# Infini-attention beside a spectral filter on one core: a causal mask moved from VectorE to TensorE, and element-wise work moved to GpSimd

## Chip, core and metric

One Trainium2 chip, one of its cores. The metric is the device time of one execution in microseconds (us), the median of several. Five engines work side by side, each through its own instructions in order: TensorE (PE; its weight loads are shown apart as PEld), VectorE (DVE), ScalarE (ACT), GpSimd (POOL) and SyncE (SP, which here only issues DMAs). PE writes to PSUM, whose tiles DVE and ACT read and GpSimd does not.

## The reference

Two independent parts, put side by side in the output of 2048 x 1152 floats.

Part A is an attention of 32 heads of 18 channels over 2048 tokens, in 4 segments of 512, with a compressive memory:

```
q,k,v = heads of x@wq, x@wk, x@wv          # 2048 x 576 each
for s in 4 segments:
    logits = qs@ks^T * 18**-0.5 + mask     # mask: -1e9 where key > query
    a_dot  = softmax(logits) @ vs
    pq     = phi(qs)                       # t>0: t+1, else exp(t)
    a_mem  = (pq@M) / (pq@z + 1e-6)
    outs  += g*a_mem + (1-g)*a_dot         # g = sigmoid(beta), per head
    M += phi(ks)^T@vs;  z += sum of phi(ks)
A = concat(outs) @ wo
```

Part B is `irfft2(rfft2(x) * (w_r + i w_i))` of a 2048 x 576 array.

## The kernel before

The program is emitted in the order in which it is to run (a manual schedule): the order of each engine's instructions is that of the Python code, and generators that `yield` are advanced in turn to interleave the work. The parts, by time in the profile: forward transform of B and projections of A (up to about 287 us), inverse transform of B with the first attention steps between (to about 388), the attention loop (to about 755), and an end with the last combination and output projection.

**Attention.** A *step* `t` is one head of one segment, 128 of them; four steps are a *round* `k` (`k,hh=divmod(t,4)`), 32 rounds; eight rounds are a segment. The softmax needs the maximum of each query row ahead of the exponential. So a step has two halves, which the loop runs ten steps apart:

- `s1(t)` (L595 to L616) computes the scores of the four blocks of 128 queries, each against the keys up to its own block: 128, 256, 384 and 512 columns, with four matmuls (L602). The tiles are `pa` (128 and 384 columns), `pc` (512) and `pb` (256), all from one PSUM pool of three buffers, `s1`. `red` (L604 to L607) then takes, on DVE, the row maxima of each of the four pieces: one custom operation adds the mask (zero, and -1e30 above the diagonal of the last 128 columns), takes the maximum and throws the sums away (`junk`); a second small instruction writes the accumulator to a column of `mg`, 128 x 4 heads x 4 blocks.
- `mpath(k)` (L617 to L632), once a round, turns `mg` into rows: a PE transpose into an `s1` buffer (`mt`, L621), two ACT copies (`mf`, and its bf16 high part `mts`, L626 and L627), a DMA from GpSimd's queue that puts the high part into a row of the stacked queries `Qs` (`put(0)`, L623), on DVE the low part (L630), and `put(1)`. In this way the maximum is subtracted by the matmul that makes the exponent.
- `s2(t)` (L633 to L658) computes the scores again, transposed, with the maxima subtracted (L641, L645, L646, L650, three PSUM tiles), and the exponentials on ACT (L642, L647, L651). At the last head of a round four selects on GpSimd (L653) clear what lies above the diagonal.
- `pv(k,jj)` (L659 on, matmul L668) multiplies the probabilities by the values, with a column of ones that gives the row sums. `u_dmas` writes both to DRAM, the row sums to `rD`.

In one pass of the loop (L828 to L867), the order is: two DMAs of waiting queues; first tile of `s1(t+10)`, first of `s2(t)`, second of `s1`, second of `s2`; `pv`; at hh=3 the low part of `mpath`; third tile of `s1`; at hh=2 the transpose of `mpath(k+2)`; third tile of `s2`; at hh=2 the ACT copies and `put(0)`; then one step of the `lane` (reciprocals) and 1.2 steps of the background list.

**Background.** `recip` (L686) loads 128 x 128 row sums (or memory denominators, `eps`), and on DVE takes the reciprocal (L695), multiplies by the gate (L696), rounds to a high part (L698) and subtracts (L699, low part); it stores both and loads them as 64 x 512. It runs seven times, the last after the loop. `den` and `mem1` compute the memory terms. `combine(g)` (L749) handles a segment's five tiles of up to 126 x 512: PE spreads the reciprocals over rows (`pb`, L765, one PSUM buffer `post`), DVE multiplies (L768, L770) and, but for the first segment, adds the memory term (L771); two passes later ACT rounds to a high part `oh` (L760) and DVE takes the low part `ol` (L761). `oproj(g)` multiplies by the output weights: eight groups of fifteen matmuls (L786) in the same PSUM buffer `post`, each evicted by ACT (L788), with a store for each two. `combine` of the first three segments lies in the loop, that of the last behind it, and it loads its tiles (`ux`, L748) through SP's queue, behind the stores of the projection before.

Of the kernel before, what the change touches and what calls it, by code (L numbers as in the profile page):

```python
# [5 lines left out]
F32=mybir.dt.float32; F32R=mybir.dt.float32r  # L6
AF=mybir.ActivationFunctionType; OP=mybir.AluOpType
# [325 lines left out]
BF=mybir.dt.bfloat16  # L333
# [34 lines left out]
class ATT:  # L368
# [174 lines left out]
    def att_setup(s,cp):  # L543
        nc,io=s.nc,s.io
        s.Qs=[cp.tile([128,8,512],BF,name=f"Qs{i}") for i in range(3)]
        s.Ks=[cp.tile([128,8,512],BF,name=f"Ks{i}") for i in range(4)]
        for i in range(4): nc.gpsimd.dma_start(s.Ks[i][108:110].rearrange("p h c -> p (h c)"),io["neg1"])
        s.mask=cp.tile([128,512],F32,name="mask"); nc.sync.dma_start(s.mask,io["mask"])
        bt=cp.tile([128,1],F32,name="bt"); nc.sync.dma_start(bt,io["beta"])
        e=cp.tile([128,1],F32,name="be"); s.gt=cp.tile([128,1],F32,name="gt"); s.g1=cp.tile([128,1],F32,name="g1")  # L550
        nc.scalar.activation(e,bt,AF.Exp,scale=-1.0)
        nc.vector.tensor_scalar(e,e,1.0,None,op0=OP.add)
        nc.vector.reciprocal(s.gt,e)
        nc.vector.tensor_scalar(s.g1,s.gt,-1.0,1.0,op0=OP.mult,op1=OP.add)
        d=lambda n,sh,dt: s.dp.tile(sh,dt,name=n)
        s.uD=[d(f"uD{i}",[576,512],F32) for i in range(4)]
        s.rD=[d(f"rD{i}",[32,512],F32) for i in range(4)]
        s.dD=[None]+[d(f"dD{i}",[32,512],F32) for i in range(1,4)]
        s.rrD=[d(f"rrD{i}",[64,512],F32) for i in range(4)]
        s.rdD=[None]+[d(f"rdD{i}",[64,512],F32) for i in range(1,4)]  # L560
# [34 lines left out]
    def s1(s,t):  # L595

        nc=s.nc; k,hh=divmod(t,4); n,qd=divmod(k,2); h=4*qd+hh
        Q,K=s.Qs[n%3],s.Ks[n%4]; tp=s.sm
        assert (n,0) in s.loaded and (n,1) in s.loaded,(t,n)
        if hh==0: s.mg[k]=tp.tile([128,4,4],F32,name="mg")  # L600
        def mm(out,i):
            nc.tensor.matmul(out,Q[:108,h,128*i:128*i+128],K[:108,h,:128*(i+1)],start=True,stop=True)  # L602
        def red(src,i):
            w=128*(i+1)  # L604
            junk=tp.tile([128,512],BF,name="junk",bufs=1)
            nc.vector.tensor_tensor_reduce(out=junk[:,:w],in0=src,in1=s.mask[:,512-w:],scale=1.0,scalar=-3.0e38,  # L606
                op0=OP.add,op1=OP.max,accum_out=s.mg[k][:,hh,i:i+1])  # L607
        pa=s.ps1.tile([128,512],F32,name="s1",tag="s1")
        mm(pa[:,:128],0); mm(pa[:,128:],2); red(pa[:,:128],0); red(pa[:,128:],2)
        yield  # L610
        pc=s.ps1.tile([128,512],F32,name="s1",tag="s1")
        mm(pc,3); red(pc,3)
        yield
        pb=s.ps1.tile([128,256],F32,name="s1",tag="s1")
        mm(pb,1); red(pb,1)
        yield  # L616
    def mpath(s,k):  # L617

        nc=s.nc; n,qd=divmod(k,2); Q=s.Qs[n%3]
        pt=s.psm.tile([128,512],F32,name="mt",tag=s.mtag)[:16,:128]  # L620
        nc.tensor.transpose(pt,s.mg.pop(k).rearrange("p h i -> p (h i)"),s.ident)  # L621
        mt=s.sm.tile([16,2,128],BF,name="mts",bufs=1)
        def put(a): nc.gpsimd.dma_start(Q[108+a:109+a,4*qd:4*qd+4].rearrange("p h (i c) -> p (h i) c",c=128),mt[:,a])  # L623
        yield
        mf=s.sm.tile([16,128],F32,name="mf",bufs=1)
        nc.scalar.copy(mf,pt)  # L626
        nc.scalar.copy(mt[:,0],mf)  # L627
        put(0)
        yield
        nc.vector.tensor_tensor(mt[:,1],mf,mt[:,0],op=OP.subtract)  # L630
        put(1)
        yield  # L632
    def s2(s,t):  # L633
# [51 lines left out]
        return L  # L685
    def recip(s,src,dst,gate,eps,load):  # L686
        nc=s.nc; tp=s.tp
        x=tp.tile([128,128],F32,name="rx",bufs=1)
        nc.sync.dma_start(x,src.rearrange("h (b c) -> (h b) c",b=4))
        yield  # L690
        yield
        yield
        if eps: nc.vector.tensor_scalar(x,x,1e-6,None,op0=OP.add)
        y=tp.tile([128,128],F32,name="ry",bufs=1)
        nc.vector.reciprocal(y,x)  # L695
        nc.vector.tensor_scalar(y,y,gate,None,op0=OP.mult)  # L696
        w=tp.tile([128,2,128],F32R,name="rw",bufs=1)
        nc.vector.tensor_copy(w[:,0],y)  # L698
        nc.vector.tensor_tensor(w[:,1],y,w[:,0].bitcast(F32),op=OP.subtract)  # L699
        nc.sync.dma_start(bass.AP(tensor=dst.tensor,offset=dst.offset,ap=[[128,128],[32*512,2],[1,128]]),w.bitcast(F32))  # L700
        yield
        yield
        r=tp.tile([64,512],F32R,name=load,bufs=1)
        nc.sync.dma_start(r.bitcast(F32),dst)
        s.rc[load]=r
        yield
# [42 lines left out]
    def combine(s,g):  # L749

        nc=s.nc; tp=s.tp; xs=s.ux
        s.oh=[None]*5; s.ol=[None]*5
        for u in range(3): s.ux_load(g,u)
        yield
        yield
        for t in range(7):
            if t>1:
                u=t-2; r=126 if u<4 else 72; x=s.am[u]
                s.oh[u]=tp.tile([126,512],F32R,name="oh",bufs=5); s.ol[u]=tp.tile([126,512],F32R,name="ol",bufs=5)
                nc.scalar.copy(s.oh[u][:r],x[:r])  # L760
                nc.vector.tensor_tensor(s.ol[u][:r],x[:r],s.oh[u][:r].bitcast(F32),op=OP.subtract)  # L761
            if t<5:
                r=126 if t<4 else 72; x=xs[t]
                pb=s.ps.tile([126,512],F32,name="pb",tag="post")
                nc.tensor.matmul(pb[:r],s.sel[:,t,:r],s.rc["rr"],start=True,stop=True)  # L765
                if g==0:
                    s.am[t]=tp.tile([126,512],F32,name="am",bufs=5)
                    nc.vector.tensor_tensor(s.am[t][:r],x[:r],pb[:r],op=OP.mult)  # L768
                else:
                    nc.vector.tensor_tensor(x[:r],x[:r],pb[:r],op=OP.mult)  # L770
                    nc.vector.tensor_tensor(s.am[t][:r],x[:r],s.am[t][:r],op=OP.add)  # L771
                if t<2: s.ux_load(g,t+3)
            yield
    def oproj(s,g):
# [15 lines left out]
                yield  # L790
    def begin(s,sm,sp,ps1):
        s.sm,s.sp,s.ps1=sm,sp,ps1
        s.mg={};s.m2={};s.P={};s.vs={};s.rc={};s.am={};s.pq={};s.ux={};s.loaded=set()
    def prologue(s):

        for n in range(2):
# [12 lines left out]
    def attention(s,tp,ps):  # L809
        s.tp,s.ps,s.psm,s.mtag=tp,ps,s.ps1,"s1"  # L810
        def steps(gen,i):
            for _ in range(i):
                try: next(gen)
                except StopIteration: return
        m=None
# [12 lines left out]
        for t in range(133):  # L828
            k,hh=divmod(t,4); n,qd=divmod(k,2); g=k//8
            if hh==0 and qd==0:  # L830
                if n+2<16: q+=s.stack_dmas(n+2,0)
                if n+3<16: q+=s.stack_dmas(n+3,1)
                if n+2<16: q.append(lambda n=n: s.load_v(n+2))
            st=t%32
            if 16<=t<21: s.pq_load(1,t-16)
            if t==34: bg.append(s.den(1,lane))
            if st==10 and g>0:
                def ln(g=g):
                    yield from s.recip(s.rD[g-1],s.rrD[g-1],s.g1,False,"rr")
                    bg.append(s.combine(g-1))  # L840
                    for u in range(5 if g<4 else 0): bg.append(s.mem1(g,u))
                    if g<3: bg.append(s.den(g+1,lane))
                    bg.append(s.oproj(g-1))
                lane.append(ln())
            a=s.s1(t+10) if t+10<128 else iter(())
            b=s.s2(t) if t<128 else iter(())
            if q: q.pop(0)()
            if qu: qu.pop(0)()
            steps(a,1)
            steps(b,1)  # L850
            steps(a,1)
            steps(b,1)
            if 4<=t-1<132: s.pv((t-5)//4,(t-5)%4)
            if hh==3 and m is not None: steps(m,1); m=None
            steps(a,1)
            if hh==2 and k+2<32: m=s.mpath(k+2); next(m)
            steps(b,1)
            if hh==2 and m is not None: steps(m,1)
            if t>=8 and t%4==0:
                s.pv_out((t-8)//4)  # L860
                if t%8==4: qu+=s.u_dmas((t-12)//8)
            for l in list(lane):
                try: next(l)
                except StopIteration: lane.remove(l)
            if q: q.pop(0)()
            if qu: qu.pop(0)()
            run_bg(1.2)  # L867
# [108 lines left out]
```

## Time and profile before

| | |
|---|---|
| median of 3 runs | 826.8 us (824.0 to 826.88) |
| profiled execution | 820.21 us, span of its instructions 818.2 us |
| mean granted TensorE clock | 0.960 |
| busy in the span | PE 727.3, DVE 611.9, ACT 472.3, POOL 181.0 us |
| masked maxima (L606) | 512 operations, 251.3 us, and 512 accumulator reads, 42.4 us |

How to read it: a row of the timeline gives start, duration, engine, line, operation, output <- inputs with shapes, and in brackets how long the engine had been idle and what ended that. Matmuls are pipelined, so their durations hold some latency and overlap; the distance between two starts says what one costs in a stream. In the view by windows, a stretch of the span has for each engine its busy time and the number of instructions. A wait is given as engine, line and tile, then what it waited for, with the sum, the number and the longest.

### The profile page before, as it was taken

Reading aid. Unit: us, or ns where it says so; the run is one execution under the profiler, and the core shown is the slowest. Engines: PE = TensorE matmul, PEld = TensorE weight load, DVE = VectorE, ACT = ScalarE, POOL = GpSimd, SP = SyncE. Lnnn points to the kernel's source line nnn. Section 1 sums busy time; section 2 is a strip of 40 time slices with the busy share of each in tenths; the row PEclk is TensorE's granted clock in tenths of the full one; section 3 lists DMA queues with packets and bytes.
Section 4 is the critical chain, followed back from the end, with each engine's and each line's share of the span. In section 5 each row is a group of like instructions: output and inputs, shape, how many; then the busy total and the mean of one; then the engine's idle time right before and its main releaser. Section 6 shows DMA issues by size and latency. Waiting matters only on the chain.

```text
span 818.2 us, 14656 instructions
## 1 busy us (share of the span) xinstructions
PE 727.3 (89%) x4751; PEld 489.2 (60%) x4751; DVE 611.9 (75%) x1687; ACT 472.3 (58%) x996; POOL 181.0 (22%) x340
## 2 busy tenths in 40 slices
PE   5998999999999969997988988899988999978856
PEld 4887788797897958895333333335542345523645
DVE  5999877895878779986788888886778767792040
ACT  2665894846846534444777755666555665657111
POOL 2110001001001164441553331331312231323000
PEclk9999999999999989999999989999996999989969
DMA  8883434653534778735576556564463644310221
GB/s 305 264 253 116 158 139 152 223 176 119 196 120 168 255 160 204 223 124 143 146 182 144 123 125 163 132 153 122 115 167 92 156 120 120 115 37 17 61 86 58
DMA packets 82496, 121.27 MB, mean 148 GB/s; under 512 B 9368, under 2 KB 49430, under 8 KB 82284
## 3 DMA queue, kind: packets, MB, share of 16 engines
q1 hardware_dynamic: 74836, 104.29, 44.2%
q0 software_dynamic: 7584, 16.05, 6.7%
q8 instruction: 38, 0.62, 0.3%
q14 instruction: 38, 0.31, 0.1%
HBM read 81.75 MB, written 38.35 MB: 147 GB/s over the span
## 4 chain that ended last, share of the span: by engine, by line
PE 60%; DVE 21%; ACT 8%; issue 6%; DMA 3%; SPq 1%; POOL 0%; DVEq 0%; ACTq 0%
PE pj L440 10%; PE po L786 8%; DVE junk L606 8%; PE s L602 8%; PE pv L668 7%; PE pjv L440 7%; PE i L292 3%; PE i L303 3%; PE s L641 2%; PE s L645 2%; PE pn L735 2%; PE pm L497 1%; DMA Qs<-qkD 1%; PE s L650 1%; DVE eo L123 1%
## 5 line engine op out<-in xcount | busy, mean ns | idle before, releaser
L606 DVE CUSTOM_DVE_ANT_0 junk<-s,mask 128x128 bf16<-128x128 f32 (+3 forms) x512 | 251.3, 491 | 71.6 <-PE s L602 27.1
L602 PE MATMUL s<-Ks,Qs 108*128 108x128 bf16 (+3 forms) x512 | 138.2, 313 | 19.5 <-DVE mg L606 16.2
L602 PEld LDWEIGHTS <-Qs 108*128 108x128 bf16 x512 | 47.1, 100 | 114.4 <-issue 100.9
L668 PE MATMUL pv<-P,vs 128*32 128x512 f32 (+3 forms) x1024 | 100.0, 463 | 1.0 <-issue 0.8
L642 ACT ACTIVATE P<-s 128x512 f32<-128x512 f32 x128 | 76.8, 600 | 41.5 <-PE s L641 34.7
L623 POOL DMA_DIRECT2D Qs<-mts x64 | 31.7, 496 | 247.3 <-ACT mts L627 184.3
L651 ACT ACTIVATE P<-s 128x256 f32<-128x256 f32 x128 | 49.1, 383 | 64.2 <-PE s L650 60.1
L647 ACT ACTIVATE P<-s 128x512 f32<-128x512 f32 x128 | 76.3, 596 | 7.5 <-PE s L646 5.6
L653 POOL TENSOR_SCALAR_AFFINE_SELECT P<-P 128x512 f32<-128x512 f32 x128 | 77.0, 641 | 14.2 <-ACT P L642 13.8
L440 PE MATMUL pj<-xh,wqkh 128*128 128x512 f32 x180 | 71.2, 395 | 0.5 <-ACT Z L151 0.5
L440 PE MATMUL pj<-xh,wqkl 128*128 128x512 f32 x180 | 71.1, 395 | 0.0
L440 PE MATMUL pj<-xl,wqkh 128*128 128x512 f32 x144 | 61.8, 429 | 0.0
L641 PE MATMUL s<-Qs,Ks 110*128 110x512 bf16 x128 | 51.2, 400 | 3.6 <-ACT P L642 2.8
L202 DVE TENSOR_TENSOR Z<-t,t 128x290 f32<-128x290 f32 (+1 forms) x96 | 53.0, 598 | 0.2
L292 PE MATMUL i<-civ,Y 128*128 128x256 f32 (+1 forms) x288 | 44.4, 308 | 9.4 <-DVE T L320 5.3
L202 DVE TENSOR_TENSOR t<-Z 128x580 f32<-128x580 f32 x64 | 48.0, 788 | 0.2
L440 PE MATMUL pjv<-wvh,xh 128*128 128x288 f32 x160 | 48.1, 303 | 0.0
L292 PEld LDWEIGHTS i<-civ,Y 128*128 128x128 f32 (+1 forms) x288 | 39.8, 199 | 11.7 <-DVE T L320 6.3
L440 PE MATMUL pjv<-wvl,xh 128*128 128x288 f32 x160 | 46.2, 295 | 0.0
L645 PE MATMUL s<-Qs,Ks 110*128 110x384 bf16 x128 | 43.5, 340 | 0.1
L606 DVE DVE_READ_ACCUMULATOR2_ANT mg<- 128x1 f32 x512 | 42.4, 83 | 0.1
L788 ACT COPY ob<-po 128x288 f32<-128x288 f32 x32 | 12.7, 398 | 48.3 <-PE po L786 48.1
(140 smaller groups left out, 1518.7 us busy)
## 6 DMA issues: line engine op xcount, KB each, us to landing
qkD<-sp SPq DMA_DIRECT2D x36, 384.0 KB
Qs<-qkD SPq DMA_DIRECT2D x96, 144.0 KB
Ks<-qkD SPq DMA_DIRECT2D x96, 144.0 KB
xin<-xb SPq DMA_DIRECT2D x16, 384.0 KB
cfw<-cfw POOLq DMA_DIRECT2D x16, 384.0 KB, 4.4
civ<-civ POOLq DMA_DIRECT2D x16, 384.0 KB, 7.1
vs<-vD SPq DMA_DIRECT2D x16, 330.0 KB
vD<-vt SPq DMA_DIRECT2D x16, 311.0 KB
```

The source lines that it names most:

```text
L202: v.tensor_tensor(o,a,b,op=op)
L292: nc.tensor.matmul(p[:m,k],Y[i][:,q,c*128:c*128+m],cc[:,hl,o:o+256],start=n==0,stop=n==5)
L440: s.nc.tensor.matmul(out,a,b,start=i==0,stop=i==len(L)-1)
L602: nc.tensor.matmul(out,Q[:108,h,128*i:128*i+128],K[:108,h,:128*(i+1)],start=True,stop=True)
L606: nc.vector.tensor_tensor_reduce(out=junk[:,:w],in0=src,in1=s.mask[:,512-w:],scale=1.0,scalar=-3.0e38, op0=OP.add,op1=OP.max,accum_out=s.m ...
L641: nc.tensor.matmul(p0,kk(0),q(0),start=True,stop=True)
L642: nc.scalar.activation(P[0][:,hh],p0,AF.Exp,scale=SC)
L645: nc.tensor.matmul(p1[:,:384],kk(1),q(128),start=True,stop=True)
L647: nc.scalar.activation(P[1][:,hh],p1,AF.Exp,scale=SC)
L653: sel=lambda x,pat: nc.gpsimd.affine_select(out=x,in_=x,pattern=pat+[[1,128]],compare_op=OP.is_ge,fill=0.0,base=0,channel_multiplier=-1)
L668: nc.tensor.matmul(s.pvt[32*hh:32*hh+32,128*j:],vt[:,j,19*h:19*h+32],mv[0][:,hh,mv[1]],start=jj==0,stop=jj==3,skip_group_check=True)
L786: nc.tensor.matmul(ps,a[t][:r,c],b[:r,t,w],start=i==0,stop=i==14)
```

## The change

1. `s1`: the score matmuls for the 384 and the 128 columns are each followed by a matmul of an identity (`idb`) with the triangle mask (`tri`, both bf16, 128 x 128), accumulated on the diagonal block. The two DVE operations on `pa` become one plain reduction, which writes the maximum of each of its four 128-column blocks to `mx`: three belong to the 384-wide piece, one to the 128-wide. The other two maxima stay as they are.
2. `mpath`: two small DVE operations in front of the transpose bring `mx` into `mg`. The low part moves from DVE to GpSimd. In the loop the transpose, the copies and `put(0)` move from hh=2 to hh=3 of the round, where they follow the four selects in GpSimd's queue, and the low part with `put(1)` from hh=3 to hh=0 of the next.
3. `recip`: works in place; multiplication and rounding go to ACT, one pass later, and the subtraction to GpSimd.
4. `combine`: the addition of the memory term and the low part go to GpSimd.

```diff
@@ att_setup
+        s.tri=cp.tile([128,128],BF,name="tri"); nc.scalar.copy(s.tri,s.mask[:,384:])
+        s.idb=cp.tile([128,128],BF,name="idb"); nc.scalar.copy(s.idb,s.ident)
@@ s1
-        if hh==0: s.mg[k]=tp.tile([128,4,4],F32,name="mg")
+        if hh==0: s.mg[k]=tp.tile([128,4,4],F32,name="mg"); s.mx[k]=tp.tile([128,4,4],F32,name="mx")
...
-        mm(pa[:,:128],0); mm(pa[:,128:],2); red(pa[:,:128],0); red(pa[:,128:],2)
+        for o,w,i in ((0,384,2),(384,128,0)):
+            mm(pa[:,o:o+w],i)
+            nc.tensor.matmul(pa[:,o+w-128:o+w],s.idb,s.tri,start=False,stop=True,skip_group_check=True)
+        nc.vector.tensor_reduce(out=s.mx[k][:,hh],in_=pa.rearrange("p (b c) -> p b c",c=128),axis=mybir.AxisListType.X,op=OP.max)
@@ mpath
+        mx=s.mx.pop(k)
+        nc.vector.tensor_reduce(out=s.mg[k][:,:,2:3],in_=mx[:,:,:3],axis=mybir.AxisListType.X,op=OP.max)
+        nc.vector.tensor_copy(s.mg[k][:,:,0:1],mx[:,:,3:])
         nc.tensor.transpose(pt,s.mg.pop(k).rearrange("p h i -> p (h i)"),s.ident)
...
-        nc.vector.tensor_tensor(mt[:,1],mf,mt[:,0],op=OP.subtract)
+        nc.gpsimd.tensor_tensor(mt[:,1],mf,mt[:,0],op=OP.subtract)
@@ recip
+        w=tp.tile([128,2,128],F32R,name="rw",bufs=1); y=w[:,1].bitcast(F32)
+        nc.sync.dma_start(y,src.rearrange("h (b c) -> (h b) c",b=4))
...
-        nc.vector.reciprocal(y,x)
-        nc.vector.tensor_scalar(y,y,gate,None,op0=OP.mult)
-        w=tp.tile([128,2,128],F32R,name="rw",bufs=1)
-        nc.vector.tensor_copy(w[:,0],y)
-        nc.vector.tensor_tensor(w[:,1],y,w[:,0].bitcast(F32),op=OP.subtract)
+        nc.vector.reciprocal(y,y)
+        yield
+        nc.scalar.activation(y,y,AF.Copy,scale=gate)
+        nc.scalar.copy(w[:,0],y)
+        nc.gpsimd.tensor_tensor(w[:,1],y,w[:,0].bitcast(F32),op=OP.subtract)
@@ combine
-                nc.vector.tensor_tensor(s.ol[u][:r],x[:r],s.oh[u][:r].bitcast(F32),op=OP.subtract)
+                nc.gpsimd.tensor_tensor(s.ol[u][:r],x[:r],s.oh[u][:r].bitcast(F32),op=OP.subtract)
...
-                    nc.vector.tensor_tensor(s.am[t][:r],x[:r],s.am[t][:r],op=OP.add)
+                    nc.gpsimd.tensor_tensor(s.am[t][:r],x[:r],s.am[t][:r],op=OP.add)
@@ attention
-            if hh==3 and m is not None: steps(m,1); m=None
+            if hh==0 and m is not None: steps(m,1); m=None
             steps(a,1)
-            if hh==2 and k+2<32: m=s.mpath(k+2); next(m)
+            if hh==3 and k+2<32: m=s.mpath(k+2); next(m)
             steps(b,1)
-            if hh==2 and m is not None: steps(m,1)
+            if hh==3 and m is not None: steps(m,1)
```

More of the change, by code (lines that the diff above doesn't have):

```diff
@@ L687, in recip @@
         nc=s.nc; tp=s.tp
-        x=tp.tile([128,128],F32,name="rx",bufs=1)
-        nc.sync.dma_start(x,src.rearrange("h (b c) -> (h b) c",b=4))
+        w=tp.tile([128,2,128],F32R,name="rw",bufs=1); y=w[:,1].bitcast(F32)
+        nc.sync.dma_start(y,src.rearrange("h (b c) -> (h b) c",b=4))
         yield
@@ L692, in recip @@
         yield
-        if eps: nc.vector.tensor_scalar(x,x,1e-6,None,op0=OP.add)
-        y=tp.tile([128,128],F32,name="ry",bufs=1)
-        nc.vector.reciprocal(y,x)
-        nc.vector.tensor_scalar(y,y,gate,None,op0=OP.mult)
-        w=tp.tile([128,2,128],F32R,name="rw",bufs=1)
-        nc.vector.tensor_copy(w[:,0],y)
-        nc.vector.tensor_tensor(w[:,1],y,w[:,0].bitcast(F32),op=OP.subtract)
+        if eps: nc.vector.tensor_scalar(y,y,1e-6,None,op0=OP.add)
+        nc.vector.reciprocal(y,y)
[3 more added lines that the diff above has]
+        nc.gpsimd.tensor_tensor(w[:,1],y,w[:,0].bitcast(F32),op=OP.subtract)
         nc.sync.dma_start(bass.AP(tensor=dst.tensor,offset=dst.offset,ap=[[128,128],[32*512,2],[1,128]]),w.bitcast(F32))
@@ L792, in begin @@
         s.sm,s.sp,s.ps1=sm,sp,ps1
-        s.mg={};s.m2={};s.P={};s.vs={};s.rc={};s.am={};s.pq={};s.ux={};s.loaded=set()
+        s.mg={};s.mx={};s.m2={};s.P={};s.vs={};s.rc={};s.am={};s.pq={};s.ux={};s.loaded=set()
     def prologue(s):
```

## Prediction

> **What bounds the kernel now.** I read the page first (shares, then the chain that ended last), then a table by stage, then single lines of the timeline. A "step" is one head in the main loop, a "round" four steps.
>
> ```profile
> PE 727.3 (89%) x4751; PEld 489.2 (60%) x4751; DVE 611.9 (75%) x1687; ACT 472.3 (58%) x996; POOL 181.0 (22%) x340
> ...
> PE 60%; DVE 21%; ACT 8%; issue 6%; DMA 3%; SPq 1%; POOL 0%; DVEq 0%; ACTq 0%
> ```
>
> PE leads the chain, DVE is second. Which of them binds changes with what runs beside the attention, so the loop (389 to 739 us) has to be cut into stretches of whole rounds. Columns: stretch, busy time of each engine, PEclk the granted clock.
>
> ```profile
> core 0: us, PE busy (x) PEld busy (x) DVE busy (x) ACT busy (x) POOL busy (x), PEclk, DMA share, GB/s
> ...
> 479.00:528.90 49.90, 41.16 (x270) 15.78 (x268) 41.72 (x152) 30.65 (x66) 13.88 (x25) 0.90 0.55 139
> 528.90:564.60 35.70, 33.97 (x242) 14.79 (x241) 27.75 (x109) 23.59 (x52) 10.16 (x19) 1.00 0.56 133
> 564.60:579.30 14.70, 12.89 (x104) 8.18 (x102) 10.83 (x36) 8.25 (x19) 3.37 (x6) 1.00 0.33 92
> 579.30:604.90 25.60, 25.21 (x193) 15.31 (x191) 18.00 (x73) 14.75 (x34) 6.72 (x12) 0.93 0.56 152
> 604.90:636.70 31.80, 25.85 (x140) 9.06 (x141) 26.44 (x84) 16.91 (x37) 7.28 (x13) 0.79 0.49 129
> 636.70:673.70 37.00, 34.92 (x251) 15.74 (x249) 26.91 (x106) 24.07 (x54) 10.12 (x18) 1.00 0.55 131
> 673.70:687.50 13.80, 11.98 (x98) 7.24 (x96) 10.86 (x36) 7.83 (x18) 3.37 (x6) 1.00 0.36 95
> 687.50:712.10 24.60, 23.96 (x192) 14.44 (x190) 17.90 (x70) 15.29 (x34) 6.41 (x12) 1.00 0.48 132
> 712.10:739.00 26.90, 20.16 (x125) 6.82 (x123) 24.11 (x59) 15.82 (x36) 7.08 (x13) 0.87 0.17 48
> ```
>
> Three kinds. **PE-bound**: the stretches from 528.9, 579.3, 636.7 and 687.5, ten rounds in 122.9 us with PE busy 94 to 98% (memory products and output projection). **DVE-bound**: those from 479.0, 604.9 and 712.1, eight rounds in 108.6 us, PE busy 75 to 82% (reciprocals and combination on DVE). The two single rounds between I leave unchanged. **Plain**: the nine rounds before 479; their length is the distance of two first P·V groups in the chain:
>
> ```profile
> 429.35 1.04 PE pv L668 x8
> 439.21 1.04 PE pv L668 x8
> ```
>
> 9.86 us, 2.465 a step. Is that DVE? A step's four masked maxima have 1280 columns:
>
> ```profile
> 430.46 0.69 DVE L606 CUSTOM_DVE_ANT_0 junk<-s,mask 128x512 bf16<-128x512 f32 x1
> ...
> 431.31 0.42 DVE L606 CUSTOM_DVE_ANT_0 junk<-s,mask 128x256 bf16<-128x256 f32 x1
> ```
>
> Start to start the 512-wide one takes 0.85. If all four fill the step, a fixed part a and a part b per column follow from 4a+1280b=2.465 and a+512b=0.85: b=1.22 ns, a=0.23 us. So the pair of 128 and 384 columns costs 2a+512b=1.08, the 256-wide 0.54, and DVE has no time left: plain rounds are DVE's.
>
> **The change, part by part.**
>
> *One plain maximum for two masked ones.* Cost of a plain 512-element operation by the distance to an independent next one:
>
> ```profile
> 786.90 0.69 DVE L771 TENSOR_TENSOR am<-ux,am 126x512 f32<-126x512 f32 x1
> 787.51 0.68 DVE L761 TENSOR_TENSOR ol<-am,oh 126x512 fp32r<-126x512 f32 x1
> ```
>
> 0.61. The trace shows no plain reduction; bounds 0.61 and 0.85, I take 0.61, since it writes no accumulator. Saved: 1.08-0.61=0.47 a step. Added per round: a reduction of 12 elements and a copy of 4, nearest row
>
> ```profile
> L552 DVE TENSOR_SCALAR be<-be x1: 153/153/153, 292.4 to 292.4; 128x1 f32<-128x1 f32 x1
> ```
>
> so 0.3 for both. DVE's plain round becomes 9.86-1.88+0.3=8.3.
>
> *Two mask matmuls a step on PE.* In the rows below 128+384 columns in two matmuls take 0.23 to the next start, 512 in one 0.22:
>
> ```profile
> 563.62 0.39 PE L602 MATMUL s<-Ks,Qs 108*128 108x128 bf16 x2
> 563.85 0.38 PE L641 MATMUL s<-Qs,Ks 110*128 110x512 bf16 x1
> 564.07 0.38 PE L602 MATMUL s<-Ks,Qs 108*128 108x512 bf16 x1
> ```
>
> So columns count and the extra weight load hides: 0.055 each (bounds 0 and 0.23), 0.43 a round. Where PE waits for DVE it is free; where PE binds it is paid.
>
> *The new wait, which I hold to be the heart of it.* The transpose of the maxima (mt) today comes at hh=2 of a round and reads maxima written a step earlier. It moves to hh=3, directly behind the fourth score matmul of that step (256 columns) on PE, and on DVE the reduction and copy that feed it stand behind that step's three maxima. PE, in order, then stands until DVE has finished the whole step; behind it wait the 256-wide probability matmul, its exponential, the selects and the next step. Today:
>
> ```profile
> PEld mt L621 <- DVE mg L606: 14.9, 20, 3.1
> ```
>
> 14.9 us in 20 of 32 places (another 10 us before the matmul itself), in DVE-bound rounds, where PE has time. The new wait in a round where DVE isn't behind, from a PE-bound step:
>
> ```profile
> 558.72 0.38 PE L602 MATMUL s<-Ks,Qs 108*128 108x512 bf16 x1
> ...
> 559.60 0.28 PE L602 MATMUL s<-Ks,Qs 108*128 108x256 bf16 x1
> ```
>
> The 512 columns stream until 558.93; a matmul's result reaches DVE some 0.4 after:
>
> ```profile
> 564.05 0.29 DVE L606 CUSTOM_DVE_ANT_0 junk<-s,mask 128x128 bf16<-128x128 f32 x1 [0.54 <-PE s L602]
> ```
>
> (563.62, 128 columns, to 564.05). So DVE starts at 559.3, ends the 512-wide at 560.15, the 256-wide at 560.7, reduction and copy at 561.0; PE, ready at 559.72, goes on at about 561.1: **1.4 us**. Bounds: nothing if DVE's work were done, 2.4 (a full step) if DVE is a step behind.
>
> What PE needs for a round without the rest: in one PE-bound round, with the 30 projection matmuls of it below,
>
> ```profile
> 662.00:673.70 11.70, 11.70 (x99) 7.24 (x97) 8.16 (x34) 7.61 (x18) 3.37 (x6) 1.00 0.40 86
> ```
> ```profile
> 662.00:673.70 11.70, 4.73 (x30) 4.11 (x30) 1.00 0.40 86
> ```
>
> 11.70-4.11=7.6. Hence:
> - Plain: 7.6+0.43+1.4 plus the first maximum waiting for PE afterwards, about 9.7 against 9.86: nine rounds give **-1** (bounds -7, DVE alone at 9.0; +6, the wait at 2.4).
> - PE-bound: +0.43+1.4 a round, less some 0.3 where DVE ends a piece of them today: ten rounds **+15** (bounds +4 and +24).
> - DVE-bound: PE's busy 87.2 holds about 1.1 a round of matmul ends behind which it waits; floor 87.2-9+8x1.83+2 (a wait for a load that stays)=95 against 108.6: **-14** (bounds -24 and -5). DVE itself loses 0.47 a step, ten additions, fifteen low parts and three operations of each reciprocal, and falls under that floor.
>
> *The prologue* holds ten of the steps beside the inverse transform: 4.7 us of DVE, mostly under PE: **-1.5** (bounds -5, +3).
>
> *Additions and low parts on GpSimd.*
>
> ```profile
> L575 POOL TENSOR_TENSOR wol<-ob,woh 126x576 fp32r<-126x576 f32 x5 | 7.0, 1408 | 5.7 <-ACT woh L574 5.7
> ```
>
> 1.25 us for 512 elements (bounds 0.69 as on DVE, 1.41). 25 of them in the loop are 31 us on an engine with some 3.4 us a round; the selects can stand behind two of them, but P·V comes two steps later: +2 (bounds 0, 15). The rows of maxima are also later: transpose a step later, and both DMA issues now stand behind the 2.4 us of selects. About 1 (ACT) + 2.4 + 0.5 + 0.3 + 0.5, and then
>
> ```profile
> DMA to landing us min/median/max: 1.5/3.7/7.2
> ```
>
> 8.4 us with the median, 11.9 with the longest, against four steps, 9.7: some rounds wait: +3 (bounds 0, 12). Together **+5**.
>
> [...]
>
> ```profile
> 735.87 2.88 DVE L761 TENSOR_TENSOR ol<-am,oh 72x512 fp32r<-72x512 f32 x1 [0.85 <-ACT oh L760]
> ```
>
> (2.88 beside the selects instead of 0.69). [...] Moving such operations off DVE gains a few of these stalls; that is in the -14.
>
> *The end*, on the path whole:
>
> ```profile
> 770.86 0.40 ACT L788 COPY ob<-po 128x288 f32<-128x288 f32 x1 [2.38 <-PE po L786]
> ```
> ```profile
> 771.60 0.95 DVE L695 RECIPROCAL ry<-rx 128x128 f32<-128x128 f32 x1 [16.34 <-DMA rx<-rD]
> ```
> ```profile
> 779.99 5.99 SPq L748 DMA_DIRECT2D ux<-uD  x5
> ```
> ```profile
> 782.68 0.69 DVE L770 TENSOR_TENSOR ux<-ux,pb 126x512 f32<-126x512 f32 x1 [9.21 <-DMA ux<-uD]
> ```
> ```profile
> 791.47 0.62 ACT L760 CAST oh<-am 72x512 fp32r<-72x512 f32 x1 [1.30 <-DVE am L771]
> ```
>
> ACT now scales and rounds the last reciprocal, in its queue before the fifth projection eviction (770.86). It must wait for 772.55, plus two small operations, 773.2; with one PSUM buffer PE waits too, the last store and the loads queued behind it on SP (779.99) slide by 2.3. Then five additions and five low parts run one after the other on GpSimd: the fifth addition is eighth, 0.75+8x1.25=10.8 after the first product, against 8.8 today (782.68 to 791.47): with its hand-overs 2.3 more. **+4.6** (bounds +1, +7).
>
> Sum: -1+15-14-1.5+5+4.6=+8.1. The profiled execution took 820.2 (span 818.2), so 828; the median of the three runs is 826.8, 0.8% above it. I carry the difference over: **834 us**.
>
> **The rivals.**
> - *DVE is done when PE arrives* (faster). If the transpose's wait stays below 0.6 us, plain rounds go to 9.0 (-8), PE-bound pay 0.43 plus 0.3 (+7), DVE-bound gain 20: -8+7-20-1.5+5+4.6=-13, 814 us. For it: DVE gets 1.9 us a round. Against: the order on both engines. The sum changes sign where the wait is about 1.1 (8.1/29 rounds below 1.4).
> - *The clock stays up* (faster). The rows show 0.90, 0.79 and 0.87 in just the three stretches where PE waits most, 15 us of lost PE clock; if shorter waits for DVE keep it at 1.00, about -15 more, 819. Against: the new wait is one more pause. [...]
> - *Late rows of maxima* (slower): if the landing is mostly late by 0.7 us in 29 rounds, 20 instead of 3: 851.
> - *No relief*: a plain maximum that costs 0.85 takes 0.24x4 from each DVE-bound or plain round's gain, about 17x0.9=15: 849.
>
> **How the numbers follow.** The forecast (825 to 845) has 0.56, the first rival 0.17, the clock 0.10, late rows 0.10, no relief 0.07. The range reaches from between the two fast rivals to the slow ones, 815 to 850. A measurement of this kernel tells about 0.5% (4 us) from no change: faster 0.25, same 0.22, slower 0.53.
>
> **What would show it.** Right: waits of mt for DVE of some 40 us in all; plain rounds of 9.6 to 9.8; stretches with projection matmuls longer by 1.5 a round, those with combination shorter by 2; 0.6 us a step for the maximum of 512; last loads of the combination issued 2 us later after the loop's end. Wrong: mt waits under 20 us, plain rounds near 9.0, or P·V waiting for the selects and the first probability matmul for the maxima's DMA by more than 10 us in all.

## The result, and the profile after

The changed kernel takes **851.3 us** (median of 4, 848.2 to 852.0), the kernel before 826.75 (4 runs beside it): ratio 1.030, 95% interval 1.025 to 1.034. The forecast was 834 with a range of 815 to 850: the sign is right, the loss is three times as large (+24.5 against +8), and the time lies 1.3 us above the range. The profiled execution took 848.2 with a span of 846.3, 28.1 more than the 818.2 of before.

First the page of the changed kernel, engines' busy time and the chain:

```profile
PE 740.8 (88%) x5007; PEld 511.8 (60%) x5007; DVE 554.9 (66%) x1279; ACT 473.5 (56%) x1012; POOL 243.5 (29%) x414
...
PE 62%; DVE 15%; ACT 7%; issue 6%; DMA 5%; POOL 3%; SPq 1%; DVEq 0%; ACTq 0%; POOLq 0%
```

DVE lost 57 us of work, as meant. PE gained only 13.5 us of busy time, but its share fell from 89 to 88% of a longer span: PE stands still more. Now the same stretches of whole rounds as in the prediction (rounds 9 to 28; columns as there):

```profile
core 0: us, PE busy (x) PEld busy (x) DVE busy (x) ACT busy (x) POOL busy (x), PEclk, DMA share, GB/s
481.10:535.30 54.20, 44.70 (x300) 18.12 (x300) 34.20 (x97) 30.51 (x70) 21.34 (x34) 0.81 0.51 126
535.30:577.30 42.00, 36.67 (x262) 15.74 (x263) 25.02 (x72) 24.91 (x54) 13.04 (x24) 0.96 0.46 117
577.30:592.50 15.20, 13.62 (x113) 8.74 (x113) 8.22 (x25) 7.57 (x18) 3.88 (x7) 1.00 0.44 117
592.50:622.50 30.00, 27.32 (x217) 17.49 (x215) 15.28 (x46) 16.61 (x40) 8.70 (x16) 0.94 0.47 117
622.50:645.30 22.80, 19.23 (x157) 8.31 (x157) 17.88 (x51) 15.18 (x35) 16.39 (x20) 1.00 0.67 170
645.30:686.40 41.10, 36.11 (x260) 15.60 (x260) 24.32 (x71) 25.17 (x55) 15.37 (x26) 1.00 0.49 122
686.40:699.80 13.40, 12.30 (x105) 7.67 (x103) 7.18 (x23) 7.58 (x18) 3.87 (x7) 1.00 0.47 133
699.80:728.60 28.80, 26.61 (x223) 17.36 (x221) 16.30 (x48) 16.74 (x40) 8.70 (x16) 1.00 0.27 80
728.60:755.10 26.50, 19.73 (x132) 7.42 (x130) 16.55 (x34) 16.02 (x37) 19.31 (x24) 0.89 0.23 68
```

The four PE-bound stretches (42.0, 30.0, 41.1, 28.8) sum to 141.9 us where they took 122.9, and PE is no longer busy 94 to 98% of them but 87 to 92%. The DVE-bound ones (54.2, 22.8, 26.5) take 103.5 after 108.6, with DVE busy only 62 to 78%: no engine is busy over 85% there any more. By the starts of the first P·V groups the whole difference divides so:

| part | before | after | difference | predicted |
|---|---|---|---|---|
| up to the first P·V | 389.4 | 392.9 | +3.5 | -1.5 |
| nine plain rounds | 89.6 | 88.3 | -1.3 | -1 |
| ten PE-bound rounds | 122.9 | 141.9 | +19.0 | +15 |
| eight DVE-bound rounds | 108.6 | 103.5 | -5.1 | -14 |
| the single rounds and the last two | 46.1 | 46.0 | -0.1 | 0 |
| end, from the last round's first P·V | 61.7 | 73.8 | +12.1 | +4.6 |

(The +5 that the prediction put on the GpSimd side, anywhere in the loop, has no row of its own.)

The view of waits says what stands, here with the us in all, the times and the longest:

```profile
PE mt L629 <- DVE mg L628: 44.4, 31, 4.9
```

The transpose of the maxima waits for DVE's copy in 31 of 32 places. One place in a PE-bound round, in order of time (the rows of DVE and two of PE; others left out):

```profile
665.14 0.68 DVE L608 CUSTOM_DVE_ANT_0 junk<-s,mask 128x512 bf16<-128x512 f32 x1
665.44 0.28 PE L604 MATMUL s<-Ks,Qs 108*128 108x256 bf16 x1
665.74 0.08 DVE L608 DVE_READ_ACCUMULATOR2_ANT mg<- 128x1 f32 x1
665.97 0.43 DVE L608 CUSTOM_DVE_ANT_0 junk<-s,mask 128x256 bf16<-128x256 f32 x1
666.32 0.08 DVE L608 DVE_READ_ACCUMULATOR2_ANT mg<- 128x1 f32 x1
666.32 0.16 DVE L627 TENSOR_REDUCE mg<-mx 128x4 f32<-128x12 f32 x1
666.40 0.28 DVE L628 COPY mg<-mx 128x4 f32<-128x4 f32 x1
666.82 0.27 PE L629 MATMUL mt<-ident,mg 128*16 128x128 f32 x1 [1.10 <-DVE mg L628]
```

PE has nothing left to do at about 665.7 and goes on at 666.8. The two operations that it waits for read `mx` of a round whose last head was done two steps earlier: they need nothing of this step. They are late only because they stand in DVE's order behind this step's 512-wide and 256-wide maxima.

Two of the waits are much longer, both in DVE-bound rounds (other rows left out):

```profile
510.25 0.69 DVE L775 TENSOR_TENSOR am<-ux,pb 126x512 f32<-126x512 f32 x1 [3.58 <-DMA ux<-uD]
...
513.02 0.37 PE L629 MATMUL mt<-ident,mg 128*16 128x128 f32 x1 [4.61 <-DVE mg L628]
```
```profile
744.29 1.26 POOL L778 TENSOR_TENSOR am<-ux,am 126x512 f32<-126x512 f32 x1
744.82 4.96 DVE L628 COPY mg<-mx 128x4 f32<-128x4 f32 x1
745.52 1.25 POOL L768 TENSOR_TENSOR ol<-am,oh 126x512 fp32r<-126x512 f32 x1
746.74 1.25 POOL L778 TENSOR_TENSOR am<-ux,am 72x512 f32<-72x512 f32 x1
747.95 1.80 POOL L661 TENSOR_SCALAR_AFFINE_SELECT P<-P 128x512 f32<-128x512 f32 x3
749.84 0.38 PE L629 MATMUL mt<-ident,mg 128*16 128x128 f32 x1 [4.89 <-DVE mg L628]
```

In the first, DVE itself waits for a load in the combination and the small operations stand behind it. In the second a copy of 4 elements, 0.16 us at its shortest, takes 4.96 while GpSimd works without a break, and ends as GpSimd's selects do (both at 749.8).

### The profile page after: what moved, and what is told of

It is laid out like the page before. It is cut to its first block, busy times and chain, and to the rows that moved or that the text cites. A ratio compares the mean times of both kernels' runs of the same rounds, so it can differ in the third digit from the quotient of the medians.

```text
span 846.3 us, 14589 instructions
## 1 busy us (share of the span) xinstructions
PE 740.8 (88%) x5007; PEld 511.8 (60%) x5007; DVE 554.9 (66%) x1279; ACT 473.5 (56%) x1012; POOL 243.5 (29%) x414
## 4 chain that ended last, share of the span: by engine, by line
PE 62%; DVE 15%; ACT 7%; issue 6%; DMA 5%; POOL 3%; SPq 1%; DVEq 0%; ACTq 0%; POOLq 0%
PE pj L440 10%; PE pv L676 9%; PE po L793 8%; PE s L604 7%; PE pjv L440 7%; DVE junk L608 4%; PE s L649 3%; PE i L292 2%; PE i L303 2%; PE s L653 2%; PE pn L742 2%; PE s L658 2%; PE s L613 1%; PE pm L497 1%; DVE mg L628 1%
## 5 line engine op out<-in xcount | busy, mean ns | idle before, releaser
L608 DVE CUSTOM_DVE_ANT_0 junk<-s,mask 128x512 bf16<-128x512 f32 (+1 forms) x256 | 141.6, 553 | 45.1 <-PE s L604 33.5
L604 PE MATMUL s<-Ks,Qs 108*128 108x384 bf16 (+3 forms) x512 | 144.7, 312 | 0.8 <-DVE mx L614 0.6
L614 DVE TENSOR_REDUCE mx<-s 128x4 f32<-128x512 f32 x128 | 88.2, 689 | 71.5 <-PE s L613 70.4
L604 PEld LDWEIGHTS <-Qs 108*128 108x128 bf16 x512 | 50.9, 99 | 90.5 <-issue 77.0
L659 ACT ACTIVATE P<-s 128x256 f32<-128x256 f32 x128 | 49.1, 384 | 89.4 <-PE s L658 88.3
L440 PE MATMUL pj<-xl,wqkh 128*128 128x512 f32 x144 | 61.7, 429 | 0.0
L202 DVE TENSOR_TENSOR t<-Z 128x580 f32<-128x580 f32 x64 | 47.9, 786 | 0.2
L629 PE MATMUL mt<-ident,mg 128*16 128x128 f32 x32 | 8.8, 277 | 44.6 <-DVE mg L628 44.4
L487 POOL MEMSET vt<- 128x32 f32 x16 | 2.3, 161 | 151.5 <-PE pm L497 85.3
L793 PE MATMUL po<-woh,oh 126*128 126x288 f32 (+1 forms) x160 | 34.0, 346 | 12.4 <-ACT ob L795 8.9
```

The costliest lines, as they stand in the source:

```text
L202: v.tensor_tensor(o,a,b,op=op)
L440: s.nc.tensor.matmul(out,a,b,start=i==0,stop=i==len(L)-1)
L614: nc.vector.tensor_reduce(out=s.mx[k][:,hh],in_=pa.rearrange("p (b c) -> p b c",c=128),axis=mybir.AxisListType.X,op=OP.max)
L793: nc.tensor.matmul(ps,a[t][:r,c],b[:r,t,w],start=i==0,stop=i==14)
```

## The experiments

Theories: **A**, the transpose's wait behind DVE's order; **B**, the moves to GpSimd and ScalarE; **C**, the 256 mask matmuls on PE; **D**, for the end, the clock. Stage times below are read like those of the table above. "Before" is the kernel before on the same chip: 826.0 us beside the first four runs, 825.8 beside the next, 824.7 beside the last.

**1 and 2. The two operations early.**

```
 # s1, behind the step's last maximum          # mpath
+if hh==3:                                     -mx=s.mx.pop(k)
+    mx=s.mx.pop(k)                            -nc.vector.tensor_reduce(out=s.mg[k][:,:,2:3],...)
+    nc.vector.tensor_reduce(...)              -nc.vector.tensor_copy(s.mg[k][:,:,0:1],mx[:,:,3:])
+    nc.vector.tensor_copy(...)
 # the first of the two runs also puts mpath back to hh==2, 2 and 3
```

> The changed kernel, but VectorE makes a round's two small operations (the late maximum over the three columns and the copy) right behind the last head's own maxima, as soon as they can run, and the mpath is issued at its old places (transpose and copies in head 2, low part's row in head 3). Nothing else differs. Theory A, the transpose's wait behind VectorE's two small operations is the main loss (1.2 to 1.3 us in nearly every round, 49.8 us of pauses ahead of the transposes against 14.1 before): the pauses fall back to about 15 us, so the time falls by 20 to 36 us, to 815 to 831. Theory B, the work moved to GpSimd and ScalarE is the main loss (end +12 us, stalled VectorE operations): at most 5 us gained, 846 to 851. Theory C, the 256 added mask matmuls on TensorE are the main loss (PE-bound rounds longer by their 0.43 us a round and the half-clock stretches): the pauses go but the time stays, 842 to 851.

> The changed kernel with the two small operations of a round made right behind the last head's own maxima; the mpath's places stay as changed (transpose in head 3, last row of maxima in head 0 of the next round). Against the run that also puts the old places back, this tells the wait from the later rows. Theory A, the wait alone: the same 815 to 831 as there, within 2 us. Rival, the later rows of maxima (ready some 2.4 us later for the second products) cost too: 5 to 10 us more than there. Theories B and C: 842 to 851.

Measured: 815.9 us (ratio 0.988, 0.983 to 0.994) with the old places, **811.9 us** (0.983, 0.979 to 0.987) with the new ones. Moving two small operations within DVE's order is worth 39 us. The second is 3 us below the range of theory A. The waits of the second run, and five of its stretches (columns as above):

```profile
PEld mt L630 <- DVE mx L614: 5.0, 4, 3.7
PE mt L630 <- DVE mx L614: 4.1, 3, 3.5
```
```profile
476.10:524.00 47.90, 41.70 (x300) 17.08 (x300) 33.05 (x97) 30.51 (x70) 20.52 (x33) 0.86 0.60 143
524.00:560.10 36.10, 34.64 (x263) 15.30 (x265) 24.21 (x72) 24.57 (x54) 13.60 (x25) 1.00 0.54 136
...
600.00:620.80 20.80, 19.21 (x153) 8.21 (x152) 17.14 (x50) 15.32 (x35) 15.51 (x19) 1.00 0.71 191
620.80:658.40 37.60, 35.90 (x264) 15.62 (x263) 24.80 (x72) 25.24 (x55) 15.81 (x27) 1.00 0.54 135
...
696.80:718.30 21.50, 18.75 (x136) 7.18 (x135) 14.23 (x34) 15.02 (x35) 15.64 (x19) 0.92 0.27 84
```

PE is back at 95% and more in the PE-bound stretches, which now take 126 us, and the DVE-bound ones (47.9, 20.8 and 21.5) 90.2. The later place of the transpose and its rows costs nothing that shows (the second run is even 4 us below the first). Only its plain rounds hold three waits of a probability matmul for the maxima's DMA, 6.1 us in all. A stands, B and C as main causes fall.

**3. Half the wait.**

```
+if hh==3 and k+2<32: s.small(k+2)     # the two operations
 steps(a,1)                            # 256-wide matmul and maximum
 if hh==3 and k+2<32: m=s.mpath(k+2); next(m)
```

> The changed kernel with a round's two small operations one part earlier in VectorE's order: ahead of the step's 256-wide masked maximum instead of behind it, so that the transpose's wait loses the 0.55 us of that maximum (about 0.7 us instead of 1.25). Theory A, the loss is proportional to the wait: 32 places by 0.55 are 17 us, 831 to 837. Rival, any pause at that place costs the same, since it is TensorE's stop and the clock behind it that count: 845 to 851.

Measured: **828.2 us** (1.004, 1.001 to 1.008), 23 below the changed kernel, more than the 17 expected. The wait in one place, and in all:

```profile
650.74 0.16 DVE L625 TENSOR_REDUCE mg<-mx 128x4 f32<-128x12 f32 x1
650.82 0.26 DVE L626 COPY mg<-mx 128x4 f32<-128x4 f32 x1
650.99 0.41 DVE L608 CUSTOM_DVE_ANT_0 junk<-s,mask 128x256 bf16<-128x256 f32 x1
651.23 0.27 PE L632 MATMUL mt<-ident,mg 128*16 128x128 f32 x1 [0.51 <-DVE mg L626]
```
```profile
PE mt L632 <- DVE mg L626: 28.9, 31, 4.9
```

44.4 became 28.9, by 15.5 us, and the loop from its first P·V to its last took 360.3 instead of 379.7: the loss goes with the wait. Another 5 us came off the end (68.8 after 73.8: two groups of the last product at half clock instead of four).

**4 to 6. The square: moves alone, mask alone, mask alone without the wait.**

```
 moves alone: the kernel before, with recip, both combination lines and mt's low part as changed
 mask alone:  the kernel changed, with  -nc.gpsimd / nc.scalar  +nc.vector  in these places
 mask early:  mask alone, with the two operations as in run 2
```

> The kernel before with only the moves between engines: the reciprocal's steps in place with gate and rounding on ScalarE and its low part on GpSimd, the combination's additions and low parts and the maxima's low part on GpSimd. Mask and maxima stay as before. Theory A, the mask part with its wait is the main loss: at most the end's own 6 us are added, 824 to 834. Theory B, the moves are the loss: 845 to 855. If the half-speed stretch of the last oproj is brought on by the moves' longer combination, its stretch from the last second product to the end is 70 us or more here, as in the changed kernel (73.8), against 61.7 before.

> The changed kernel with the moves taken back: reciprocal, combination and the maxima's low part all on VectorE as before (the reciprocal still in place). Mask by TensorE, one plain maximum and the two small operations stay. Theory A: the loop loses as in the changed kernel and the end is as before, 836 to 846. Theory B: the loss goes, 815 to 830. If the two halves add up, this run's difference to before and that of the moves alone sum to +24 to +25 us.

> The run of the mask part alone (851.1 us) with the two small operations made right behind the last head's own maxima. Completes the square of mask part and moves without the wait. Theory A: the wait alone is worth 36 to 40 us whatever else is moved, so 811 to 816, and the mask part without its wait gains 10 to 15 us on the kernel before. Rival, the early operations only help because the moves relieve VectorE: 825 to 840.

| us | DVE keeps the work | work moved |
|---|---|---|
| mask on DVE | 826 | 817.0 (0.989, 0.982 to 0.996) |
| mask on PE, operations late | 851.1 (1.029, 1.025 to 1.034) | 851.3 |
| mask on PE, operations early | 812.7 (0.983, 0.976 to 0.990) | 811.9 |

The moves alone gain 9 us, which neither theory had (824 to 834 and 845 to 855); the mask part alone loses 25, more than expected, and gains 13 without its wait. The wait costs 38 to 39 us in either column, and with it or without it the moves add nothing to the mask part in the whole time. The expectation that the two halves add up fell.

In the loop they do add up. From the first P·V to the last round it takes 367.2 us before, 357.7 with the moves, 357.8 with the mask part early and 347.9 with both. What the moves gain there they give back in the end, 62.3 without and 74.9 with them. Why the moves alone still gain isn't settled: their profile is of the slowest of four executions (811.9 to 823.8 us), with an end of 72.5.

**7. Each mask matmul twice.**

```
-nc.tensor.matmul(pa[...],s.idb,s.tri,start=False,stop=True,...)
+for _ in range(2): nc.tensor.matmul(pa[...],s.idb,s.tri,start=False,stop=True,...)
```

> The run with the early small operations (811.9 us) with each of the 256 mask matmuls issued twice (the mask is added twice; the sums stay far below every score). This measures theory C, what one set of 256 mask matmuls costs on TensorE: if it all lies on the path, 8 a round at the 0.054 us by which the prediction priced them, 0.43 us a round or 14 us, 824 to 828; if only TensorE-bound rounds pay, 5 to 6 us, 816 to 819; nothing: 810 to 814.

Measured: 819.2 us (10 executions), 7.3 above run 2. Rounds 13 to 18 and 21 to 26 take 78.7 and 78.6 us instead of 76.0 each: 5.3 in twelve rounds, 0.44 a round against the 0.43 by which the prediction priced them. In plain rounds that nothing else lengthens they cost 0.26 (8.65 instead of 8.39 us), in the last two nothing. C is real, and small.

**8 and 9. The end on VectorE**, on top of run 2: first only the last combination, then the last reciprocal too.

```
 # combine                                  # recip, last one only
+eng=nc.vector if g==3 else nc.gpsimd       -yield; nc.scalar.activation(...); nc.scalar.copy(...); nc.gpsimd...
-nc.gpsimd.tensor_tensor(s.ol[u]...)        +nc.vector.tensor_scalar(y,y,gate,...); nc.vector.tensor_copy(w[:,0],y)
+eng.tensor_tensor(s.ol[u]...)              +nc.vector.tensor_tensor(w[:,1],y,...)
```

> The run with the early small operations (811.9 us) with only the last combination's additions and low parts on VectorE; the last reciprocal keeps its steps on ScalarE and GpSimd and its extra yield. With the run that takes both back this splits the end. If the combination's moves are the larger part (2.2 us of chain and the half-speed product behind it): 803 to 807. If the reciprocal's are: 809 to 812.

> The run with the early small operations (811.9 us) with the end as before: for the last reciprocal and the last combination alone, VectorE does gate, rounding and low part, the additions and the low parts, with one yield fewer. From the last round of P.V to the end that run took 74.9 us, the kernel before 61.7, the run with the mask part alone 63.7. Theory B for the end (the moves themselves lengthen it, by +4.3 for the chain up to the last eviction, +2.2 for the combination and some +5 for the last product at half speed): the stretch falls back to 62 to 64 us and the time to 799 to 803. Rival (the half-speed last product comes whatever the engines, and the chain through DRAM hides the reciprocal): 808 to 812.

Measured: 808.7 us (0.982, 0.977 to 0.987), between the two expectations, and **804.4 us** (0.976, 0.970 to 0.981), 1.4 above the expected range. The end goes from 74.9 to 70.2 to 66.3: 4.7 for the combination, 3.9 for the reciprocal. So the two are about equal. It doesn't reach 62 to 64, since the loop now leaves it 1.8 us more of the segment before (the eighth eviction comes 24.4 us into the end; before, 22.6) and the wait ahead of the second spreading matmul is 4.4 instead of 3.3 us.

**10 to 12. Keeping the clock up.**

```
+def warm(n):
+    d=s.ps1.tile([128,512],F32,name="s1",tag="s1")
+    for _ in range(n): nc.tensor.matmul(d,s.Ks[0][:108,0,:128],s.Ks[0][:108,0,:],start=True,stop=True)
 # combine(3): warm(a) ahead of it, warm(b) in each step t
```

> The run with the early small operations (811.9 us) with matmuls added that nobody reads: 8 ahead of the last combination and 3 in each of its 7 steps, 108 by 128 and 108 by 512 bf16, into a free PSUM tile. Theory D, the last product's first groups run at half the clock because TensorE paused in the combination (four groups of 4.4 us against 2.75): they run at 2.75 us and the time falls by 4 to 7 us, 805 to 808. Rival, those groups are slow for another reason, or the added matmuls stand in the way of the combination: 811 to 816.

> The run with the last reciprocal and combination on VectorE (804.4 us) with matmuls that nobody reads, 14 ahead of the last combination, 4 in each of its first five steps and 5 in each of its last two. With the additions on GpSimd the same idea held the clock at 1.00 through the combination, but TensorE then waited for the last high and low parts and the clock was at half for the product all the same. Theory D: now the waits are short enough, the last product's groups take 2.75 us from the first on, and the last part, from the last high part to the end, falls from 28.4 to 26 us and the combination from 13.0 to 12: 799 to 803. Rival, a pause of about 1 us in the combination is enough for half speed: 803 to 808.

> As the run with idle matmuls and the end on VectorE, with 18 ahead of the combination and 3 in each of its 7 steps, to tell whether the long pause ahead of the combination (4.4 us) or the short ones within (0.8 to 1.3 us) bring on the half speed. If the long one: clock at 1.00 throughout, 799 to 803. If the short ones: half speed from the middle of the combination on, 803 to 808.

Measured: 813.5 (805.7 to 813.9), **803.4** (0.973, 0.967 to 0.978) and 804.7 us. First the end without the idle matmuls (run 9), cut at the eighth eviction, at the fifth high part and some 9 us behind it; then with them (run 11; columns as above):

```profile
737.00:761.40 24.40, 21.04 (x152) 16.84 (x152) 2.23 (x5) 3.41 (x9) 0.04 (x1) 1.00 0.20 64
761.40:774.90 13.50, 4.26 (x8) 1.95 (x9) 8.55 (x14) 2.94 (x6) 0.00 (x0) 0.65 0.34 109
774.90:784.00 9.10, 8.08 (x34) 7.17 (x34) 1.16 (x2) 1.32 (x3) 0.00 (x0) 0.59 0.00 0
```
```profile
740.10:764.60 24.50, 21.16 (x153) 17.06 (x154) 2.33 (x5) 3.38 (x9) 0.13 (x1) 1.00 0.20 64
764.60:777.50 12.90, 12.10 (x50) 4.78 (x49) 8.40 (x14) 2.87 (x5) 0.00 (x0) 1.00 0.34 114
777.50:786.50 9.00, 7.39 (x50) 6.47 (x49) 1.29 (x2) 1.82 (x4) 0.00 (x0) 1.00 0.08 33
```

With PE kept busy (12.10 of 12.90 us in the combination, where it was 4.26 of 13.50) the clock stayed at 1.00, and the last product's groups take 2.75 us from the first on, 50 matmuls in 9 us instead of 34. D is shown for these two runs: the half speed came with PE's standing. The idle matmuls delay nothing that shows: the combination's first product starts 28.8 us into the end (29.1 without them). So the profiled end is 3.4 us shorter (62.9 after 66.3), but the median falls by 1.0 us only, with executions from 801.0 to 807.6 without and from 800.3 to 804.9 with them: the gain in time isn't settled. In the run with the additions on GpSimd (run 10, above the expected 805 to 808) the clock held through the combination and fell right when the last product began: 0.50 from 779.4 on, behind 3.00 us in which PE was busy for 0.67. With 18 and 3 idle matmuls (run 12) it was 0.51 in the 3 us from 774.7, near the combination's end, behind 3.00 us in which PE was busy for 1.91: in this run the short pauses were enough.

The best version is run 9 or, within the noise, run 11: 803 to 804 us, 2.4 to 2.7% below the kernel before.

## Why the prediction was right in sign and wrong in size

- **The wait (1.4 us a place, about 40 us in all): right.** The view's brackets have 1.1 in nearly every round. Counted as in the prediction, from where the matmul before has streamed its columns (665.44 and 0.11 for 256 columns, in the rows above), it is 1.27. In all it is 44.4 in the waits' view, and run 2 gains 39.4 without it. Runs 1 to 3 show it to be the cause. The first rival of the prediction, "DVE is done when PE arrives" (814), is what comes out in the total once DVE may do the two operations early (811.9); its parts don't fit, since it put the end at +4.6 and run 2 has +13.2.
- **Plain rounds (-1): right**, -1.3: five of 9.4 us, three of 9.8 and one of 11.6 (10.5 before). Their 7.6 us of PE was 11.70 less the weight loads' column (4.11); with the matmuls' own (4.73) it would be 7.0. The regular plain rounds of run 2 take 8.39, so 7.6 was rather low already.
- **PE-bound rounds (+15): +19.0.** Run 2 takes 125.9 us here, so the wait is 16.0 of it, 1.6 a round; between the two runs of the mask part alone it is 13.0 (135.8 and 122.8, the latter as long as before in spite of the mask matmuls). In the changed kernel two of these stretches were granted a clock of 0.96 and 0.94, in run 2 all have 1.00. The mask matmuls cost 0.44 a round in run 7. The runs don't divide the other 3 us further.
- **DVE-bound rounds (-14): -5.1, the largest miss. The step that failed is the floor of 95**: PE's own work, 2 us for a load that stays, and 8x1.4=11.2 for the waits. Run 2 divides the miss. Without the late operations these rounds take 90.2, so the wait costs 13.3 here, 2.1 more than priced. The larger part is there without it: 90.2 against 95-11.2=83.8. In the three stretches of run 2 shown above PE is busy 79.7 us and stands 10.5, where the floor had 2. The longest stop there (other rows left out):

```profile
503.77 0.69 DVE L776 TENSOR_TENSOR am<-ux,pb 126x512 f32<-126x512 f32 x1 [5.85 <-DMA ux<-uD]
505.12 0.38 PE L630 MATMUL mt<-ident,mg 128*16 128x128 f32 x1 [3.47 <-DVE mx L614]
```

 DVE waits for the combination's load and the transpose for DVE, with the two operations early too; the kernel before has no such wait in the loop. Rounds 9 to 11, up to the end of the one with this load, take 36.9 us before, 39.5 in the changed kernel and 36.6 in run 2. Of DVE's wait for it the mask part alone with early operations has 1.8 us and the moves alone 3.9; whether the load comes later, by the reciprocal's extra pass, or DVE only reaches it sooner stays open. The rest of PE's 10.5 us is mostly the spreading matmul, which waits for DVE's multiplications (3.9) and for the reciprocals' load (1.9). The second long stop of the changed kernel, the 4-element copy, does go with the early operations.
- **The prologue (-1.5): +3.5.** I gave the wait no place there. Three transposes come before the first P·V, with gaps of 1.6, 0.1 and 1.6 us in the view (before: 0, 0 and 0.8). With late operations the prologue takes 392.9 to 393.5 us in three runs, with early ones 387.5 to 391.7 in nine. The remainder of the difference isn't settled.
- **GpSimd's side (+5): nothing in the changed kernel.** No probability matmul waits for the rows of maxima in the changed kernel; P·V's loads wait 2.3 us for selects (before: 4.7). GpSimd's additions and low parts took 1.27 us each, as priced. So the rival "late rows" (851), which would give the time measured, is not what happened; nor is "no relief": the plain maximum goes by in 0.60 us, start to start. Once PE no longer stands, the later rows do show (run 2: 6.1 us in three waits).
- **"The clock stays up" (819) did not come either.** The DVE-bound stretches were granted 0.81, 1.00 and 0.89 (before: 0.90, 0.79 and 0.87, and 0.93 in one PE-bound stretch).
- **The end (+4.6): +12.1, the second step that failed: it had no term for the clock.** The rows of the changed kernel:

```profile
789.05 0.40 ACT L704 ACTIVATE rw<-rw,g 128x128 f32<-128x128 f32 x1 [3.06 <-DVE rw L702]
789.49 0.30 ACT L705 CAST rw<-rw 128x128 fp32r<-128x128 f32 x1
789.69 0.39 ACT L795 COPY ob<-po 128x288 f32<-128x288 f32 x1
...
790.14 1.57 PE L793 MATMUL po<-woh,oh 126*128 126x288 f32 x5 [1.85 <-ACT ob L795]
```
```profile
799.40:815.00 15.60, 5.22 (x9) 2.24 (x9) 3.43 (x5) 3.37 (x6) 10.42 (x9) 0.64 0.30 95
815.00:831.00 16.00, 14.27 (x55) 13.23 (x56) 0.00 (x0) 1.32 (x4) 1.93 (x2) 0.50 0.05 18
```

 The eviction waits behind the reciprocal's two steps as foreseen, and PE behind it for 1.85 us; the next group then runs at half clock (4.2 us between evictions instead of 2.8). Up to the combination's first product that makes 4.9 us where 2.3 were priced. 1.3 of them is the wait behind the reciprocal, 1.4 the half clock and 0.6 the load; 1.6 is there already at the fourth eviction, ahead of the reciprocal's steps (13.1 us into the end, 11.5 before). The second chain is as priced: the fifth high part comes 10.99 us after the first product (10.8 foreseen; 8.79 before). Then 16 us of the last product run at 0.50, where before only the first group did: 5.0 us more from there to the end.
- **The sum.** Misses of +9 (DVE-bound), +7.5 (end), +5 (prologue), +4 (PE-bound) and -5 (GpSimd's side) make the 20 us by which +28.1 stands above +8.1. The runs divide it in another way too. The wait was priced at 27x1.4=38 us in the three kinds of rounds and costs 39.4. So what failed is what the rest of the change was to gain: 796 us follow from the forecast without the wait, 811.9 were measured (run 2). The prediction also put the change of sign at a wait of 1.1 us; counted like its 1.4, run 3 still waits 0.67 in most rounds and is 0.4% slower than before.

## What to carry to other kernels

An engine that runs in order made two small operations as late as everything that stood ahead of them: PE waited 44.4 us for them in 31 places. Before moving a consumer, look at where its producer stands in the *other* engine's order, and put the producer right behind the data that it needs: here that turned +3% into -1.7%. Price a new wait also for the moments in which the engine waited for is itself held up, and for the clock behind it. Before crediting the relief of a busy engine, ask what it will wait for next: here a load (5.85 us in run 2). Moving work off a busy engine gained here in the loop, where that engine binds (357.8 to 347.9 us with the operations early), and lost in the end, where a chain runs alone (62.3 to 74.9), so decide it stage by stage: here GpSimd in the loop, VectorE at the end.

## What the runs showed of the hardware that was not expected

- **The clock halved after a pause of 1.85 us** (granted 0.51 in the 3.5 us behind it), and it stayed at half through 16 us of dense matmuls (815.0 to 831.0 above: PE busy 89%, granted 0.50). In run 9 it came back some 8 us into the last product (0.50 up to 782.0, 0.94 in the 3 us behind).
- **Stops of similar length ended differently.** In run 10 PE was busy for 1.08 of the 3.00 us from 752.4 on, and the next 3 us were granted 0.51; it was busy for 1.35 of the 3.00 us from 767.4 on, and the next 6 us were granted 1.00. Nor did busy matmuls bring the clock back at once: in the changed kernel it stayed at 0.50 from 513.6 to 527.2, with PE busy for all of these 13.6 us. What decides between these cases isn't settled.
- **A 4-element copy on DVE took 4.96 us beside GpSimd.** In the run of the mask part alone, with the operations as late and without GpSimd's added work, the longest of the 32 copies took 0.58 us, in the changed kernel 4.96. With early operations it was 0.24 without that work and 2.94 with it (run 2). The 32 copies take 13.8 us in the changed kernel and 9.4 in the mask part alone.
